# Sixteen weight clamps on POOL, and the partition swaps of one token block as products with an exchanged unit matrix

## The chip, the cores and the metric

The kernel runs on one core of a Trainium2 chip. The metric is device time in microseconds (us) of one launch, the median of several runs. The engines are PE (matrix products, with a queue of its own for weight loads, PEld), DVE, ACT and POOL (elementwise work and reductions), and SP, which here only issues transfers. Each engine works through its own instructions strictly in the order in which the program lists them, and an instruction that waits for another engine holds up everything behind it on its own.

## The reference

```python
def _attn_ref(q, k, v):                      # 8 batches, 8 heads, 576 tokens, head size 64
    q_s = q - np.max(q, axis=-1, keepdims=True)
    q_s = np.exp(q_s)
    q_s = q_s / (np.sum(q_s, axis=-1, keepdims=True) + 1e-09)
    k_s = k - np.max(k, axis=2, keepdims=True)
    k_s = np.exp(k_s)
    k_s = k_s / (np.sum(k_s, axis=2, keepdims=True) + 1e-09)
    kv = np.einsum('bhsd,bhse->bhde', k_s, v)
    return np.einsum('bhsd,bhde->bhse', q_s, kv)

def reference(...):                          # x: 4608 tokens x 512
    x = attn_out.transpose(0, 2, 1, 3).reshape(B * S, H * D)
    x = relu(x @ w_in) ** 2 @ w_out          # 512 -> 2048 -> 512
    return relu(x @ w_in2) ** 2 @ w_out2     # the same with other weights
```

## The kernel before

The 4608 tokens are cut into 9 blocks j of 512. Linear attention gives each block its x in four parts p (two heads each), and x meets the first weight matrix in 16 chunks f per block; such a chunk is one `h_mm`, twelve products of 128x512. From block 6 on, and in the three later matrix stages, the products are combined in a seven-product scheme instead (stages 2 to 4 of the program). All products use numbers split in a high and a low part, so each operand needs an ACT instruction (high part) and a DVE instruction (low part) before PE can use it.

**Weights of the first layer** (`first_weights`, f = 0 to 15) arrive as 64-bit floats and are put together from two 32-bit words: `load_raw` (transfer on SP, line 137), `low_word` (ACT, line 153), `high_word` (a clamp, line 157), `scaled` (ACT, line 162), `join` (DVE, line 167), then `w_hi` (ACT) and `w_lo` (DVE) split them. The raw words of nine weights lie in three rooms (w5, w6, w7); the other seven reuse these places once a join has freed one.

**Attention of block j, part p** (`attend`): for the keys `k_max` (DVE, lines 313 to 315), `k_all` (a maximum over all partitions on POOL, line 319), `k_sub` (DVE, line 323), `k_exp` (ACT, line 326), `kv_mm` (PE, line 334), `kv_whole` (ACT, line 353). For the queries, from block 1 on, a head's 64 numbers lie on two neighbouring groups of 32 partitions, so maxima and sums of each half must be exchanged between the groups: `q_max` (DVE), `q_swap` (four copies of 32x16 on ACT, line 362), `q_max2` and `q_sub` (DVE), `q_exp` (ACT), `q_sum` (DVE), `s_swap` (again four copies on ACT), `q_norm` and `q_turn` (DVE), and `x_mm` (PE, line 405).

**The order** is not the code's order. Every step is entered with a due time, a cost and the places that it uses (a buffer or one of eight PSUM banks, `ps`); `schedule` plays these through once and writes down, engine by engine, in what order the steps would start. `search` first tries 400 random changes of the early due times on ACT and DVE and keeps those by which chunk 8 of block 2 starts earlier in that plan. So a change of one step's engine or cost reorders everything in the first 200 us.

Of the kernel before, what the change touches and what calls it, by code (L numbers as in the profile page):

```python
# [14 lines left out]
ALU = mybir.AluOpType  # L15
# [33 lines left out]
def linear_attention_two_relu2_ffn(ctx: ExitStack, tc: tile.TileContext, q0, k0, eye, qh, kh, vh, wio, out):  # L49
# [104 lines left out]

    def high_word(f, a, h):
        low, high, byte = views(f, a, h)
        nc.vector.tensor_scalar(out=high, in0=high, scalar1=W_MAX, scalar2=-W_MAX, op0=ALU.min, op1=ALU.max)

    def scaled(f, a, h, new):
        wfs[f, a, h] = new()  # L160
# [196 lines left out]
    def swap(name, src):  # L357
# [4 lines left out]
            nc.scalar.activation(out=t[o:o + 32], in_=src[i:i + 32], func=AF.Copy)  # L362
        return t

    def q_max(j, p):
        m = qmt[j, p] = pool.tile([P, 16, 1], F32, name=f"qm{j}_{p}", tag="qm")
        nc.vector.tensor_reduce(out=m, in_=qt[j, p], axis=AX.X, op=ALU.max)

    def q_swap(j, p):
        qmo[j, p] = swap(f"qmo{j}_{p}", qmt[j, p])  # L370

    def q_max2(j, p):
        m = qmt[j, p]
# [10 lines left out]
        s = qmt[j, p] = pool.tile([P, 16, 1], F32, name=f"qs{j}_{p}", tag="qs")  # L384
        nc.vector.tensor_reduce(out=s, in_=qt[j, p], axis=AX.X, op=ALU.add)

    def s_swap(j, p):
        qso[j, p] = swap(f"qso{j}_{p}", qmt[j, p])

    def q_norm(j, p):  # L390
        q, s = qt[j, p], qmt.pop((j, p))
# [370 lines left out]
    def converted(f, a, h, due, raw, wf):  # L762

        (rp, rnew), (wp, wnew) = raw, wf
        l = dma(due - 8000, lambda: load_raw(f, a, h, rnew), 512, [], [rp], held=10000 if (f, a) == (3, 0) else None)
        late = 2500 if f else 0
        c = op("ACT", act(512) + 40, due - 3000, lambda: low_word(f, a, h), [l], [rp], lag=late)
        g = op("DVE", 430, due - 2900, lambda: high_word(f, a, h), [l], [rp], lag=late, port=True)
        x = op("ACT", act(512) + 40, due - 1900, lambda: scaled(f, a, h, wnew), [g], [rp, wp])
        return op("DVE", 690, due - 700, lambda: join(f, a, h), [c, x], [rp, wp], port=True)  # L770

# [121 lines left out]
    def attend(j, p):  # L893
# [31 lines left out]
        if j == 0:  # L925
            l = start_loads[p]
            mq, sq, qT = Place("qm"), Place("qs"), Place(f"q{p % 2}", parent=qspace)
            bq = Place("ps")
            y = op("DVE", 690, d - 13500, lambda: max0(p), [l["q"]], [mq, room])
            y = op("POOL", gps(400), d - 12500, lambda: sub0(p), [y], [mq, room])  # L930
            y = op("ACT", act(512), d - 10500, lambda: qexp0(p), [y], [room])
            y = op("DVE", 690 + 160 + 250 + 690, d - 9500, lambda: q_norm0(p), [y], [sq, room], port=True)
            y = op("PE", 700, d - 8000, lambda: q_turn0(p, bq), [y, start_eye], [bq, room, beginroom])
            turned.append(y)
            qe = op("ACT", act(512, 1), d - 6500, lambda: q_out0(p, qnew), [y], [qT, bq])
            nm = op("DVE", 360, d - 6000, lambda: kv_norm(0, p), [kvmm], [s, ps])
            wh = kv_done[0, p] = op("ACT", 660, d - 5000, lambda: kv_whole(0, p), [nm, start_eye], [s, ps, beginroom])
            xlast = op("PE", 1150, d - 3000, lambda: x_mm0(p, xb), [wh, qe], [xb, qT, beginroom])
        else:
            q = Place(f"q{side}", parent=qroom)  # L940
            lq = dma(d - 30000, lambda: load_q(j, p, qnew), 256, [], [q])
            qm, qo, qs, so = Place("qm"), Place("qmo"), Place("qs"), Place("qso")
            qT = Place("qT")
            y = op("DVE", 690, d - 22000, lambda: q_max(j, p), [lq], [qm, q])
            y = op("ACT", 900, d - 21000, lambda: q_swap(j, p), [y], [qo, qm])
            y = op("DVE", 170, d - 19500, lambda: q_max2(j, p), [y], [qm, qo], port=True)
            y = op("DVE", dve(512), d - 19000, lambda: q_sub(j, p), [y], [q, qm], port=True)
            y = op("ACT", act(512), d - 17500, lambda: q_exp(j, p), [y], [q])
            y = op("DVE", 690, d - 16000, lambda: q_sum(j, p), [y], [qs, q])
            y = op("ACT", 900, d - 14500, lambda: s_swap(j, p), [y], [so, qs])  # L950
            y = op("DVE", 170 + 250 + 690, d - 13000, lambda: q_norm(j, p), [y], [q, qs, so], port=True)
            y = op("DVE", 710, d - 11500, lambda: q_turn(j, p), [y], [qT, q])
            if own:
                nm = op("DVE", 360, d - 8500, lambda: kv_norm(j, p), [kvmm], [s, ps])
                kv_done[j, p] = op("ACT", 660, d - 7500, lambda: kv_whole(j, p), [nm, start_eye, blank[0], x_done.get((j - 1, p))], [s, ps, beginroom])
            xlast = op("PE", 1250, d - 5500, lambda: x_mm(j, p, xb), [y, kv_done[j - 1, p], kv_done.get((j, p))], [xb, qT, beginroom], lag=SLACK)
            x_done[j, p] = xlast
# [13 lines left out]
    def inner(j, kk, d):  # L971
        quad = Place("qc")
        copies = [op("ACT", act(512, 1), d - 5500 - 12000 * (i == 0), lambda i=i: v_copy(j, kk, i), [halves[j, kk + 2 * i][0]], [quad, halves[j, kk + 2 * i][1]]) for i in range(2)]
        combine(f"v{j}_{kk}", v_rooms[j % 2][kk], d, ("DVE",) * 3, lambda: vq[j, kk], quad, copies, *cf_place("cf"))

    blank = [None]

    def blank_unit():
# [2 lines left out]
    for j in range(NB):  # L981
        for p in range(NP):
            plan(when(0, j) - 25000 - (3 - rank(j, p)) * 12500, lambda j=j, p=p: attend(j, p))
        if j == 0:
            plan(when(0, 0) - 25000, blank_unit)


    stored, y_stored, chunks = {}, {}, {}
# [253 lines left out]
```

## Time and profile before

| what | value |
|---|---|
| median of 3 runs | 1509.36 us (1506.9 to 1509.76) |
| the profiled execution | 1511.11 us, of which the trace's span is 1509.3 us |
| PE busy over the span | 1487.6 us, 99% |
| DVE, ACT, POOL busy | 79%, 64%, 17% |
| granted TensorE clock | 0.999 |

PE is nearly always busy, so the time is PE's work plus the gaps in it. Nearly all gaps lie in the first 62 us; there DVE and ACT are as full as PE, and the transfers too. A line such as L157 is the line of the kernel before; in the changed kernel the lines of the second part stand 13 to 23 lines further down.

### The profile page before, as it was taken

Reading aid. Unit: us, or ns where it says so; the run is one execution under the profiler, and the core shown is the slowest. Engines: PE = TensorE matmul, PEld = TensorE weight load, DVE = VectorE, ACT = ScalarE, POOL = GpSimd, SP = SyncE. Lnnn points to the kernel's source line nnn. Section 1 sums busy time; section 2 is a strip of 40 time slices with the busy share of each in tenths; the row PEclk is TensorE's granted clock in tenths of the full one; section 3 lists DMA queues with packets and bytes.
Section 4 is the critical chain, followed back from the end, with each engine's and each line's share of the span. In section 5 each row is a group of like instructions: output and inputs, shape, how many; then the busy total and the mean of one; then the engine's idle time right before and its main releaser. Section 6 shows DMA issues by size and latency. Waiting matters only on the chain.

```text
span 1509.3 us, 30549 instructions
## 1 busy us (share of the span) xinstructions
PE 1487.6 (99%) x12036; PEld 1414.4 (94%) x12036; DVE 1190.4 (79%) x1823; ACT 971.0 (64%) x1617; POOL 253.6 (17%) x193
## 2 busy tenths in 40 slices
PE   6999999999999999999999999999999999999998
PEld 5788888789999999999999999999999999999998
DVE  7998777899867999999986455444456999999996
ACT  8987767787765666666654788787777443444442
POOL 1001000000110111111113153243311111111110
PEclk9999999999999999999999999999999999999999
DMA  9888989986759444444447677677669644444441
GB/s 368 287 292 319 342 319 336 346 295 204 228 189 328 167 146 138 140 139 140 140 139 273 222 233 257 206 259 249 197 202 325 207 146 136 138 137 138 138 137 55
DMA packets 154144, 326.63 MB, mean 216 GB/s; under 512 B 13072, under 2 KB 84880, under 8 KB 151184
## 3 DMA queue, kind: packets, MB, share of 16 engines
q1 hardware_dynamic: 152128, 300.83, 59.5%
q0 software_dynamic: 1872, 23.86, 4.4%
q8 instruction: 94, 1.54, 0.4%
q14 instruction: 50, 0.41, 0.1%
HBM read 189.63 MB, written 135.00 MB: 215 GB/s over the span
## 4 chain that ended last, share of the span: by engine, by line
PE 90%; DMA 3%; ACT 3%; DVE 2%; issue 1%; POOL 1%; SPq 0%; DVEq 0%; ACTq 0%; POOLq 0%
PE y L448 44%; PE m L448 22%; PE h L448 15%; PE n L448 5%; PE xps L405 2%; PE kvps L334 1%; DMA qx<-w 1%; DMA W<-o 1%; POOL touch L188 0%; ACT w L153 0%; ACT wf L162 0%; DMA w<-w 0%; DMA w<-wio 0%; DMA qc<-w 0%; DMA att<-vh 0%
## 5 line engine op out<-in xcount | busy, mean ns | idle before, releaser
L448 PE MATMUL y<-G,W 128*128 128x256 f32 x3024 | 345.3, 277 | 2.0 <-DVE t L488 2.0
L448 PE MATMUL m<-x,W 128*128 128x256 f32 x3024 | 345.7, 277 | 1.5 <-DMA W<-o 1.5
L448 PEld LDWEIGHTS y<-G,W 128*128 128x128 f32 x3024 | 344.8, 188 | 2.2 <-DVE t L488 2.2
L448 PEld LDWEIGHTS m<-x,W 128*128 128x128 f32 x3024 | 345.1, 188 | 1.7 <-DMA W<-o 1.7
L448 PE MATMUL y<-W,G 128*128 128x256 f32 x3024 | 343.9, 276 | 0.0
L448 PEld LDWEIGHTS y<-W,G 128*128 128x128 f32 x3024 | 343.7, 188 | 0.0
L448 PE MATMUL h<-hl,w 128*128 128x512 f32 x1080 | 259.9, 396 | 3.4 <-DVE w L84 3.4
L448 PEld LDWEIGHTS h<-hl,w 128*128 128x128 f32 x1080 | 200.4, 188 | 49.6 <-DVE w L84 5.7
L479 POOL TENSOR_TENSOR ts<-ts,ts 128x512 f32<-128x512 f32 x61 | 93.5, 1533 | 750.2 <-DVE t L518 460.4
L119 ACT ACTIVATE G<-hl 128x1280 fp32r<-128x1280 f32 (+1 forms) x95 | 86.4, 926 | 115.9 <-PE y L448 65.5
L488 DVE TENSOR_TENSOR t<-m,ts 128x512 f32<-128x512 f32 x72 | 49.1, 688 | 97.5 <-PE m L448 77.9
L125 DVE TENSOR_TENSOR G<-hl,G 128x512 fp32r<-128x512 f32 (+1 forms) x95 | 108.7, 1149 | 16.2 <-ACT G L119 15.2
L448 PE MATMUL n<-v,W 128*128 128x256 f32 x1008 | 120.3, 280 | 0.0
L448 PEld LDWEIGHTS n<-v,W 128*128 128x128 f32 x1008 | 117.1, 188 | 2.1 <-issue 1.7
L491 ACT ACTIVATE t<-t 128x512 f32<-128x512 f32 x96 | 59.8, 628 | 56.2 <-DVE t L488 51.8
L494 ACT ACTIVATE t<-t 128x512 f32<-128x512 f32 x144 | 88.5, 627 | 2.3
L125 DVE TENSOR_TENSOR G<-cf,G 128x1280 fp32r<-128x1280 f32 x51 | 79.7, 1562 | 7.9 <-ACT G L119 7.3
L125 DVE TENSOR_TENSOR G<-att,G 128x1280 fp32r<-128x1280 f32 x49 | 75.9, 1549 | 8.4 <-ACT G L119 7.6
L319 POOL PARTITION_ALL_REDUCE m<-m x28 | 27.0, 964 | 310.5 <-DVE m L315 187.0
L435 ACT ACTIVATE r<-h 128x512 f32<-128x512 f32 x96 | 56.8, 593 | 20.6 <-PE h L448 14.8
L521 POOL TENSOR_TENSOR t<-t,t 128x512 f32<-128x512 f32 x34 | 61.0, 1817 | 42.0 <-DVE t L488 42.0
L119 ACT ACTIVATE G<-cf 128x1280 fp32r<-128x1280 f32 x51 | 64.5, 1265 | 5.6 <-DVE cf L106 5.5
(199 smaller groups left out, 1888.5 us busy)
## 6 DMA issues: line engine op xcount, KB each, us to landing
g<-t SPq DMA_DIRECT2D x192, 256.0 KB, 4.0
hl<-g SPq DMA_DIRECT2D x51, 512.0 KB, 3.8
raw<-wio SPq DMA_DIRECT2D x48, 512.0 KB, 5.3
g<-r SPq DMA_DIRECT2D x96, 256.0 KB, 5.2
W<-o POOLq DMA_DIRECT2D x13, 1792.0 KB, 9.5
y<-t SPq DMA_DIRECT2D x72, 256.0 KB, 2.4
w<-wf SPq DMA_DIRECT2D x64, 256.0 KB, 5.4
o<-S SPq DMA_DIRECT2D x9, 1792.0 KB, 8.3
```

The costliest lines, as they stand in the source:

```text
L119: nc.scalar.activation(out=low[key] if x == 0 and key in low else hls[key][:, 0, r], in_=src, func=AF.Copy)
L125: nc.vector.tensor_tensor(out=hl[:, 1, r], in0=src, in1=f32(hi), op=ALU.subtract)
L319: nc.gpsimd.partition_all_reduce(m[:, 1, :P], m[:, 0, :P], P, bass.bass_isa.ReduceOp.max)
L334: nc.tensor.matmul(ps[j * D:(j + 1) * D, 0:D + 1], k[lo:, c, j * D:(j + 1) * D], v[lo:, c, j, :], start=(c == 0), stop=(c == KC - 1),)
L405: nc.tensor.matmul(ps[:, r], begin[b % 2][p], q[:, r], start=True, stop=True)
L435: nc.scalar.activation(out=r0[j, f].rearrange("p a b -> p (a b)"), in_=m.pop(("h", j, f)), func=AF.Relu)
L448: nc.tensor.matmul(ps, a, b, start=start, stop=True, skip_group_check=True)
L479: (nc.gpsimd if eng == "POOL" else nc.vector).tensor_tensor(out=t[k, "s5"], in0=t[k, "s5"], in1=t[k, "s2"], op=ALU.add)
L488: nc.vector.tensor_tensor(out=temp(k, q), in0=m[k, i], in1=t[k, "s5"], op=ALU.add)
L491: nc.scalar.activation(out=t[k, q], in_=t[k, q], func=AF.Relu)
L494: nc.scalar.activation(out=t[k, q], in_=t[k, q], func=AF.Square)
L521: nc.gpsimd.tensor_tensor(out=t[k, q], in0=t[k, q], in1=t[k, o], op=ALU.add)
```

## The change

Two things. The clamp `high_word` of the first layer's sixteen weights runs on POOL instead of DVE (the other 48 clamps stay on DVE). And in block 1 alone, the exchange of neighbouring partition groups for maxima and sums is done by PE: a product with a unit matrix whose groups of 32 columns are exchanged (`turn`), into a PSUM bank that DVE then reads, in place of four ACT copies each. The exchanged unit matrix is built on POOL by four copies when the unit matrix has landed (`turn_unit`).

```diff
--- before.py
+++ after.py
@@ -154,7 +154,7 @@
 
     def high_word(f, a, h):
         low, high, byte = views(f, a, h)
-        nc.vector.tensor_scalar(out=high, in0=high, scalar1=W_MAX, scalar2=-W_MAX, op0=ALU.min, op1=ALU.max)
+        (nc.vector if f else nc.gpsimd).tensor_scalar(out=high, in0=high, scalar1=W_MAX, scalar2=-W_MAX, op0=ALU.min, op1=ALU.max)
 
     def scaled(f, a, h, new):
         wfs[f, a, h] = new()
@@ -362,12 +362,25 @@
             nc.scalar.activation(out=t[o:o + 32], in_=src[i:i + 32], func=AF.Copy)
         return t
 
+    turned_unit = []
+
+    def turn_unit(new):
+        t = new()
+        turned_unit.append(t)
+        for g in range(4):
+            nc.gpsimd.tensor_copy(t[:, 32 * g:32 * g + 32], unit[0][:, 32 * (g ^ 1):32 * (g ^ 1) + 32])
+
+    def turn(name, src, place):
+        t = wide(place, name)[:, :16]
+        nc.tensor.matmul(t, turned_unit[0], src.rearrange("p a b -> p (a b)"), start=True, stop=True)
+        return t.rearrange("p (a b) -> p a b", b=1)
+
     def q_max(j, p):
         m = qmt[j, p] = pool.tile([P, 16, 1], F32, name=f"qm{j}_{p}", tag="qm")
         nc.vector.tensor_reduce(out=m, in_=qt[j, p], axis=AX.X, op=ALU.max)
 
-    def q_swap(j, p):
-        qmo[j, p] = swap(f"qmo{j}_{p}", qmt[j, p])
+    def q_swap(j, p, place):
+        qmo[j, p] = turn(f"qmt{j}_{p}", qmt[j, p], place) if place else swap(f"qmo{j}_{p}", qmt[j, p])
 
     def q_max2(j, p):
         m = qmt[j, p]
@@ -384,8 +397,8 @@
         s = qmt[j, p] = pool.tile([P, 16, 1], F32, name=f"qs{j}_{p}", tag="qs")
         nc.vector.tensor_reduce(out=s, in_=qt[j, p], axis=AX.X, op=ALU.add)
 
-    def s_swap(j, p):
-        qso[j, p] = swap(f"qso{j}_{p}", qmt[j, p])
+    def s_swap(j, p, place):
+        qso[j, p] = turn(f"qst{j}_{p}", qmt[j, p], place) if place else swap(f"qso{j}_{p}", qmt[j, p])
 
     def q_norm(j, p):
         q, s = qt[j, p], qmt.pop((j, p))
@@ -765,7 +778,7 @@
         l = dma(due - 8000, lambda: load_raw(f, a, h, rnew), 512, [], [rp], held=10000 if (f, a) == (3, 0) else None)
         late = 2500 if f else 0
         c = op("ACT", act(512) + 40, due - 3000, lambda: low_word(f, a, h), [l], [rp], lag=late)
-        g = op("DVE", 430, due - 2900, lambda: high_word(f, a, h), [l], [rp], lag=late, port=True)
+        g = op("DVE", 430, due - 2900, lambda: high_word(f, a, h), [l], [rp], lag=late, port=True) if f else op("POOL", 1000, due - 3600, lambda: high_word(f, a, h), [l], [rp], port=False)
         x = op("ACT", act(512) + 40, due - 1900, lambda: scaled(f, a, h, wnew), [g], [rp, wp])
         return op("DVE", 690, due - 700, lambda: join(f, a, h), [c, x], [rp, wp], port=True)
 
@@ -939,15 +952,17 @@
         else:
             q = Place(f"q{side}", parent=qroom)
             lq = dma(d - 30000, lambda: load_q(j, p, qnew), 256, [], [q])
-            qm, qo, qs, so = Place("qm"), Place("qmo"), Place("qs"), Place("qso")
+            qm, qs = Place("qm"), Place("qs")
+            by = j == 1
+            qo, so = (Place("ps"), Place("ps")) if by else (Place("qmo"), Place("qso"))
             qT = Place("qT")
             y = op("DVE", 690, d - 22000, lambda: q_max(j, p), [lq], [qm, q])
-            y = op("ACT", 900, d - 21000, lambda: q_swap(j, p), [y], [qo, qm])
+            y = op("PE", 200, d - 21000, lambda: q_swap(j, p, qo), [y, unit_turned[0]], [qo, qm, unit_place]) if by else op("ACT", 900, d - 21000, lambda: q_swap(j, p, None), [y], [qo, qm])
             y = op("DVE", 170, d - 19500, lambda: q_max2(j, p), [y], [qm, qo], port=True)
             y = op("DVE", dve(512), d - 19000, lambda: q_sub(j, p), [y], [q, qm], port=True)
             y = op("ACT", act(512), d - 17500, lambda: q_exp(j, p), [y], [q])
             y = op("DVE", 690, d - 16000, lambda: q_sum(j, p), [y], [qs, q])
-            y = op("ACT", 900, d - 14500, lambda: s_swap(j, p), [y], [so, qs])
+            y = op("PE", 200, d - 14500, lambda: s_swap(j, p, so), [y], [so, qs, unit_place]) if by else op("ACT", 900, d - 14500, lambda: s_swap(j, p, None), [y], [so, qs])
             y = op("DVE", 170 + 250 + 690, d - 13000, lambda: q_norm(j, p), [y], [q, qs, so], port=True)
             y = op("DVE", 710, d - 11500, lambda: q_turn(j, p), [y], [qT, q])
             if own:
@@ -973,6 +988,13 @@
         copies = [op("ACT", act(512, 1), d - 5500 - 12000 * (i == 0), lambda i=i: v_copy(j, kk, i), [halves[j, kk + 2 * i][0]], [quad, halves[j, kk + 2 * i][1]]) for i in range(2)]
         combine(f"v{j}_{kk}", v_rooms[j % 2][kk], d, ("DVE",) * 3, lambda: vq[j, kk], quad, copies, *cf_place("cf"))
 
+    unit_place = Place("turn", parent=raw_rooms[0])
+    unit_turned = [None]
+
+    def plan_turn():
+        unit_turned[0] = op("POOL", 900, -70000, lambda: turn_unit(lambda: raw_rooms[0].area(3072, P)), [start_eye], [beginroom, unit_place], port=False)
+        turned.append(unit_turned[0])
+
     blank = [None]
 
     def blank_unit():
@@ -983,6 +1005,7 @@
             plan(when(0, j) - 25000 - (3 - rank(j, p)) * 12500, lambda j=j, p=p: attend(j, p))
         if j == 0:
             plan(when(0, 0) - 25000, blank_unit)
+            plan(-80000, plan_turn)
 
 
     stored, y_stored, chunks = {}, {}, {}
```

On POOL, the part between the reset of the unit matrix (`begin`) and the key maxima of block 1 (`m_0` to `m_3`, one for each part p) stood as follows; a row `ISA` that names no tile sets POOL's configuration for the kind of instruction that follows.

```order
L979 MEMSET begin 128x128
L319 ISA
L319 ISA m_0_579<-m_0_579 128x128
L319 ISA m_1_623<-m_1_623 128x128
L319 ISA m_2_782<-m_2_782 128x128
```

In the changed kernel (L157 is the clamp; w_0_222, w_0_251 and w_0_262 are the rooms w5, w6, w7 with the raw words), from the tenth clamp on:

```order
L157 TENSOR_SCALAR w_0_222<-w_0_222 128x512
L319 ISA
L319 ISA m_0_569<-m_0_569 128x128
L157 ISA
L157 TENSOR_SCALAR w_0_222<-w_0_222 128x512
L319 ISA
L319 ISA m_1_589<-m_1_589 128x128
L157 ISA
L157 TENSOR_SCALAR w_0_222<-w_0_222 128x512
L157 TENSOR_SCALAR w_0_251<-w_0_251 128x512 x3
L157 TENSOR_SCALAR w_0_262<-w_0_262 128x512
L319 ISA
```

The first key maximum is now behind the tenth clamp, the second behind the eleventh, the third behind five more, and where one such row served all 28 key maxima, five now stand between the tenth clamp and the third maximum.

On DVE, around the second `k_sub` (`att_2_423` holds the keys of part 1; `qm`, `qs` are maxima and sums, `qmt` the exchanged maxima in PSUM), before:

```order
L315 TENSOR_TENSOR m_1_623<-m_1_623,att_2_432 128x128
L367 TENSOR_REDUCE qm_1_628<-qx_318 128x16
L385 TENSOR_REDUCE qs_0_632<-qx_318 128x16
L157 TENSOR_SCALAR w_0_233<-w_0_233 128x512
L323 TENSOR_TENSOR att_2_432<-att_2_432,m_1_623 128x640
```

and now:

```order
L315 TENSOR_TENSOR m_1_589<-m_1_589,att_2_423 128x128
L323 TENSOR_TENSOR att_2_364<-att_2_364,m_0_569 128x640
L380 TENSOR_REDUCE qm_0_608<-qx_325 128x16
L323 TENSOR_TENSOR att_2_423<-att_2_423,m_1_589 128x640
L387 TENSOR_TENSOR qm_0_608<-qm_0_608,qmt_0_617 128x16
L391 TENSOR_TENSOR qx_325<-qx_325,qm_0_608 128x512
L380 TENSOR_REDUCE qm_1_638<-qx_325 128x16
L398 TENSOR_REDUCE qs_0_644<-qx_325 128x16
```

The sums `qs_0` stood ahead of the second `k_sub` (L323) and now stand behind it. ACT's matching steps have moved the same way: `k_exp` of part 1 now stands directly ahead of `q_exp` of part 0.

On PE, after the first chunks of block 0 (`h_...`), the exchange products L375 of the changed kernel:

```order
L461 MATMUL h_4_593<-hl_0_379,w_0_508 128x512 x9
L461 MATMUL h_4_593<-hl_0_475,w_0_508 128x512 x3
L375 MATMUL qmt_0_617<-qm_0_608,w_0_222 128x16
L461 MATMUL h_5_619<-hl_0_379,w_0_508 128x512 x9
L461 MATMUL h_5_619<-hl_0_475,w_0_508 128x512 x3
L334 MATMUL kvps_0_648<-att_2_364 64x65 x10
L375 MATMUL qst_0_661<-qs_0_644,w_0_222 128x16
L375 MATMUL qmt_1_669<-qm_1_638,w_0_222 128x16
L461 MATMUL h_6_674<-hl_0_379,w_0_562 128x512 x9
```

Eight such products are new; `qst_0` stands behind six chunks and one `kv_mm`, and everything else of PE behind it. Before, `kv_mm` of part 0 was followed by a chunk.

## Rows read from the trace of the kernel before

**Rows 1.** The page's head: busy time and share of each engine.
```profile
span 1509.3 us, 30549 instructions
PE 1487.6 (99%) x12036; PEld 1414.4 (94%) x12036; DVE 1190.4 (79%) x1823; ACT 971.0 (64%) x1617; POOL 253.6 (17%) x193
```
**Rows 2.** Busy time in three stretches: length, PE, PEld, DVE, ACT, POOL, clock, DMA.
```profile
0.00:26.55 26.55, 15.50 (x124) 10.29 (x124) 19.43 (x45) 19.31 (x40) 5.44 (x11) 1.00 0.94 351
26.55:62.00 35.45, 33.14 (x168) 24.81 (x168) 31.84 (x69) 33.20 (x75) 2.44 (x3) 1.00 0.95 356
62.00:110.00 48.00, 47.99 (x288) 38.20 (x289) 46.46 (x103) 42.60 (x107) 3.51 (x4) 1.00 0.77 260
```
**Rows 3.** PE in order of time: start, us, what, and the wait before it.
```profile
26.55 5.78 PE L448 MATMUL h<-hl,w 128*128 128x512 f32 x24 [1.53 <-DVE w L84]
32.64 11.17 PE L448 MATMUL h<-hl,w 128*128 128x512 f32 x48 [0.31 <-DVE w L84]
43.74 0.95 PE L334 MATMUL kvps<-att 128*64 128x65 f32 x20
44.62 3.02 PE L448 MATMUL h<-hl,w 128*128 128x512 f32 x12
48.44 0.43 PE L405 MATMUL xps<-qT,begin 128*128 128x64 f32 x2
```
**Rows 4.** DVE's clamps, grouped, in the first 110 us; and in two stretches.
```profile
L157 DVE TENSOR_SCALAR w<-w 128x512 f32<-128x512 f32 x16 | 6.2, 420 | 0.0
0.00:26.55 26.55, 2.19 (x6) 1.00 0.94 351
26.55:62.00 35.45, 4.13 (x11) 1.00 0.95 356
```
**Rows 5.** One of ACT's swaps (line 362), four copies.
```profile
38.17 0.89 ACT L362 ACTIVATE qmo<-qm 32x16 f32<-32x16 f32 x4 [0.62 <-DVE qm L367]
```
**Rows 6.** POOL in order of time.
```profile
0.73 0.52 POOL L1165 MEMSET begin<- 128x512 f32 x1 [0.29 <-POOLq L1234]
1.19 0.42 POOL L1166 MEMSET begin<- 128x384 f32 x1
5.82 1.05 POOL L263 TENSOR_TENSOR w<-w,mq 128x512 f32<-128x512 f32 x1 [4.21 <-DVE mq L255]
21.91 0.20 POOL L979 MEMSET begin<- 128x128 f32 x1 [5.89 <-PE qps L299]
39.34 0.73 POOL L319 PARTITION_ALL_REDUCE m<-m  x1 [17.22 <-DVE qm L374]
42.69 0.70 POOL L319 PARTITION_ALL_REDUCE m<-m  x1 [2.62 <-DVE m L315]
```
**Rows 7.** POOL's sequencer at lines 263, 319 and 479: duration, first and last start.
```profile
L263 POOLq MODIFY_POOL_CONFIG  x2: 11/14/16, 1.8 to 1.8; - x2
L319 POOLq MODIFY_POOL_CONFIG  x2: 11/11/11, 22.1 to 22.1; - x2
L479 POOLq MODIFY_POOL_CONFIG  x2: 88/88/88, 359.6 to 359.6; - x2
```
**Rows 8.** SP's issue of the tenth raw weight, and issues with KB, us to landing.
```profile
26.26 0.33 SPq L137 DMA_DIRECT2D w<-wio  x1
w<-wio SPq DMA_DIRECT2D x1, 512.0 KB, 7.0
raw<-wio SPq DMA_DIRECT2D x48, 512.0 KB, 5.3
begin<-eye SPq DMA_DIRECT2D x1, 64.0 KB, 1.8
```
**Rows 9.** DVE and ACT in order of time around the first key maximum.
```profile
38.82 0.29 DVE L315 TENSOR_TENSOR m<-m,att 128x128 f32<-128x128 f32 x1
40.10 0.83 DVE L323 TENSOR_TENSOR att<-att,m 128x640 f32<-128x640 f32 x1 [0.83 <-POOL m L319]
40.84 0.68 DVE L378 TENSOR_TENSOR qx<-qx,qm 128x512 f32<-128x512 f32 x1
40.96 0.74 ACT L326 ACTIVATE att<-att 128x640 f32<-128x640 f32 x1 [0.71 <-DVE att L323]
41.60 0.61 ACT L381 ACTIVATE qx<-qx 128x512 f32<-128x512 f32 x1
```
**Rows 10.** Small products and weight loads on PE, grouped.
```profile
L405 PE MATMUL xps<-qT,begin 128*128 128x64 f32 x8 | 1.5, 273 | 0.0
L299 PEld LDWEIGHTS qps<-begin,w x16: 139/142/231, 10.7 to 21.5; 128*128 128x128 f32 x16
```

## The prediction

> **What bounds the kernel now.** I read the page's head first: PE is busy for 1487.6 of 1509.3 us [rows 1]. The three stretches then show where its gaps are: 11.05 us of them before the first chunk at 26.55, 2.31 us from there to 62, and 0.01 us from 62 to 110 [rows 2]. After 62 us nothing but PE's own work counts. Before it, DVE and ACT are nearly full (31.84 and 33.20 of 35.45 us between 26.55 and 62), and so are the transfers (0.95) [rows 2]; POOL, with 2.44 us, is empty there. PE in order of time says what the gaps wait for: weights' low parts from DVE [rows 3]. So the change can save at most the gaps before 62 us, and it can cost whatever it makes PE wait.
>
> **What it removes.** Sixteen clamps of 0.42 us leave DVE: 2.19 us before the first chunk and 4.13 us (with one clamp of a later layer, which stays) up to 62 [rows 4]. Eight swaps of 0.89 us leave ACT [rows 5]. Neither engine ends the span; the relief is worth, at most, the waits that it shortens. Of the 2.31 us of gaps after the first chunk, 0.31 lie before 43.74 [rows 2, 3]; I let the other 2.0 vanish, since both reliefs are larger: −2.0. Before the first chunk I count nothing: the chain there goes through ACT, which does the same low words, scalings and high parts as before.
>
> **What it adds on PE.** Eight products with 16 columns. The nearest row has 64 columns: four `x_mm` pieces, two records each, 1.5 us, so 0.37 each; the floor is two weight loads of 0.14, 0.28 [rows 10]. I take 0.33, and 0.3 for the first, which stands inside the sum below: 0.3 and 7 × 0.33 = +2.3.
>
> **What it adds on POOL.** A one-input instruction over 128x512 is not in the trace on POOL. Writing alone (memset) takes 0.52, two inputs take 1.05 [rows 6]; I take 0.8 for a clamp. Ten clamps at 0.8 are hidden: their words arrive before 34 us, and POOL did nothing between 22.1 and 39.34 [rows 6]. The four copies that build the exchanged matrix wait for the unit matrix (issued about 0.7, 1.8 us to land [rows 8]), so the first subtraction on POOL moves back. With 0.2 per copy (a memset of this width took 0.20 [rows 6]) POOL is free at 3.3 instead of 1.6. If the configuration then takes the 4.0 us priced below, the subtraction starts at 7.4 instead of 5.82; ACT's exponential of it would wait some 0.7. Bounds 0 and 0.7; I take +0.4.
>
> **The switches.** Each row without a tile in POOL's order appears in the trace as MODIFY_POOL_CONFIG: before the first elementwise instruction (1.8 us), before the first key maximum (22.1) and before the first sum of a later stage (359.6) [rows 7]. Their own 11 to 88 ns say nothing of how long POOL then can't work. What bounds it: the first instruction behind it began at 5.82, so the first switch took at most 4.0 us; the second at most 17.2 (22.1 to 39.34) [rows 6, 7]. The lower bound is nothing, since in each case the operand came last and hid the switch. The changed order has five switches between the tenth clamp and the third key maximum, two of them between the first and the second maximum, each with work waiting. I price one by the tighter row, 4.0, stretched by 7.0/5.3, the time in which the same 512 KB load lands in this crowded stretch against its median [rows 8], as code has to be fetched too: 5.3 us. Ends: 0 and 17.2.
>
> The Trainium skill has a rule on just this: "GPSIMD Engine Reference", section "2.1 Instruction dispatch", says that the first call of a freshly loaded kernel on POOL additionally pays about 6 us (measured there as 5.95), with no instruction of its own in a profile. Rows 6 contradict it as a fixed price, since the first switch here fitted into 4.0; by 5.95 the sum below would be +13.3 instead of +11.4.
>
> **The walk.** The tenth raw weight is issued at 26.26 and lands 7.0 later, at 33.3 [rows 8]; its clamp ends at 34.1. The switch behind it ends at 34.1 + 5.3 = 39.4. The operand of the first maximum is ready as before (39.1 [rows 9]), so the first maximum starts at 39.4, as before (39.34). It lasts 0.73 [rows 6]. Then come switch, clamp, switch: 5.3 + 0.8 + 5.3. The second maximum starts at 51.5, where it started at 42.69 before [rows 6]. Behind it, from the first maximum's rows: DVE's `k_sub` begins 0.76 after the maximum's start (39.34 to 40.10), occupies DVE for 0.74, and ACT's `k_exp` begins 0.86 after it [rows 9]. The order now puts the first part's `q_max2`, `q_sub`, `q_sum` on DVE behind this `k_sub`, and `q_exp` on ACT behind this `k_exp`. So: `k_sub` at 52.3, `q_max2` 53.0, `q_sub` 53.2 to 53.9, `q_exp` to 54.5, `q_sum` to 55.3. PE's `qst_0` needs that sum. PE reaches it after six chunks (43.74 before [rows 3]), one `kv_mm` of 0.88 and `qmt_0` of 0.3: at 44.9. It waits 55.3 − 44.9 = +10.4, with everything behind it.
>
> What is late next? DVE and ACT have been held at the same place for about as long, so the three start again together. The next two switches and five clamps end at 51.5 + 0.73 + 5.3 + 5 × 0.8 + 5.3 = 66.8, for the third maximum. DVE gets to its operand 36 instructions behind `k_sub`; at 31.84/69 = 0.46 each [rows 2] that is 52.3 + 16.6 = 68.9: hidden, by 2 us. The clamp that ACT needs first is ready at 59.1, and ACT gets there 18 instructions at 0.44 [rows 2] behind `k_exp`, at 61: hidden too. Without that cover (a switch over 7 us) the third wait comes on top.
>
> **Sum.** 0.3 + 10.4 + 2.3 − 2.0 + 0.4 = +11.4 us. The profiled execution took 1511.11, which gives 1522.5; the median of the runs lies 1.75 lower, so 1509.4 + 11.4 = **1520.8** is what I forecast for the median. A switch of 2.5 us gives a second maximum at 45.9 and +5.6, so 1515; one of 8 us moves the first maximum to 42.1, the second to 59.6, and gives +19.5, so 1529.
>
> **Rivals.**
> *Long switches.* All 16 DMA engines are full while the switches run [rows 2], and the only row under such load allows up to 17.2 us. At 12 us the first maximum starts at 46.1, the second at 71.6, PE goes on at 75.4: a wait of 30.5, +31.5, 1541. For it speaks the load, against it the 4.0 of the first switch.
> *Cheap switches.* The trace never shows POOL waiting for one. At 1 us the second maximum starts at 42.8 and PE waits 1.7: +2.3, 1511.7. No change then, unless PE, now in line behind DVE's maxima and sums at eight places, waits some 1 us at six of them: 1517.
> *Faster.* The switches cost at most 0.4 us each, and the relief reaches PE whole: all 2.31 us of gaps and the 2.19 us of clamps before the first chunk vanish, and the products cost one exposed weight load of 0.14 each, 1.1: −3.4, 1506.0. It decides from the price of a switch alone: above 0.4 us the second maximum is later than PE needs it. DVE at 90% and ACT at 94% speak for some such gain [rows 2]; against it, a PE that had only 2.31 us to gain there.
>
> **Chances.** Switches of 2.5 to 8 us: 0.58 (1514 to 1529). Long ones: 0.15. Cheap ones: 0.17 (1508.5 to 1517), of which a good 0.04 end over 0.2%. Faster: 0.10. What a measurement of this kernel can tell from no change is about 0.2%, 3 us; so faster 0.09, same 0.14, slower 0.77. The range of 1509 to 1535 leaves out most of the faster case and the upper two thirds of the long switches, together about 0.2.
>
> **What would show it.** Right: more MODIFY_POOL_CONFIG rows on POOL between 33 and 70 us, some 5 us of nothing behind each although its operand is there; the second maximum near 51; PE idle for about 10 us before a product of line 375, released by DVE's `qs`; DVE and ACT idle at the same time; after 75 us the same rows as before, shifted. Wrong: the second maximum near 42 and no gap there; or gaps of over 8 us, with a second stall at the third maximum. Were the gap there and the total still small, the start before 26.55 must have become shorter, which I gave nothing.

## The result, and the profile after

| | before | after |
|---|---|---|
| median of 4 runs each, us | 1508.39 (1506.90 to 1509.76) | 1525.62 (1523.36 to 1527.61) |
| ratio, 95% interval | 1 | 1.0102 [1.0071, 1.0133] |
| the profiled execution, us | 1511.11, span 1509.3 | 1527.28, span 1525.3 |

The change costs 1525.62 − 1508.39 = 17.2 us by the medians, and 1508.39 × 0.0102 = 15.4 us by the ratio. The forecast was 1520.8. Slower was right, by the mechanism forecast, and inside the range; the size was too small. Beside each of the later experiments, 4 of the 15 to 19 runs of the kernel before lie at 1515.6 to 1520.9 us, at no lower clock and from no known cause; ratios and medians differ there by up to 0.24%.

Busy time of the changed kernel in the middle stretch of [rows 2] and in three short ones within it (length, PE, PEld, DVE, ACT, POOL, clock, DMA share, GB/s):

```profile
26.55:62.00 35.45, 21.30 (x96) 16.11 (x94) 14.59 (x29) 16.57 (x32) 4.39 (x5) 0.81 0.60 231
35.00:43.00 8.00, 5.15 (x23) 3.94 (x21) 3.62 (x9) 3.04 (x6) 0.00 (x0) 1.00 1.04 391
43.00:51.00 8.00, 5.50 (x14) 4.23 (x14) 1.42 (x2) 2.26 (x4) 0.73 (x2) 0.63 0.49 191
51.00:57.50 6.50, 1.55 (x21) 1.03 (x20) 0.00 (x0) 0.00 (x0) 0.65 (x2) 0.76 0.00 0
```

Between 26.55 and 62 us PE is busy for 21.30 us, where it was 33.14 [rows 2]. DVE and ACT have fallen with it, from 31.84 and 33.20 to 14.59 and 16.57, and the transfers from 0.95 to 0.60. POOL gained only 1.95 us of busy time. So all engines stood still together, for something that counts as nobody's work: between 51 and 57.5 us DVE and ACT have not one instruction, and not a byte moves. POOL in order of time, from the tenth clamp on (compare [rows 6]):

```profile
33.76 1.12 POOL L157 TENSOR_SCALAR w<-w 128x512 f32<-128x512 f32 x1 [5.91 <-ACT w L222]
43.18 0.72 POOL L319 PARTITION_ALL_REDUCE m<-m  x1 [8.30 <-DMA w<-wio]
50.99 0.64 POOL L157 TENSOR_SCALAR w<-w 128x512 f32<-128x512 f32 x1 [7.09 <-issue]
57.49 0.72 POOL L319 PARTITION_ALL_REDUCE m<-m  x1 [5.86 <-issue]
65.08 3.55 POOL L157 TENSOR_SCALAR w<-w 128x512 f32<-128x512 f32 x5 [6.87 <-issue]
78.65 0.99 POOL L319 PARTITION_ALL_REDUCE m<-m  x1 [10.03 <-DVE m L315]
```

"<-issue" means that POOL waited for nothing that the profile shows. Each such gap has a row of POOL's sequencer at its start. At lines 157 and 319 (first and last start at the right):

```profile
L157 POOLq MODIFY_POOL_CONFIG  x4: 98/98/98, 43.9 to 58.2; - x4
L319 POOLq MODIFY_POOL_CONFIG  x6: 1/33/36, 34.8 to 68.8; - x6
```

Four switches stand between the tenth clamp and the five later ones: 8.30, 7.09, 5.86 and 6.87 us. The 8.30 is put down to a transfer, but the operand of the first maximum was ready at 38.06, and that of the second at 39.05, when DVE's last steps on them ended. The second maximum starts at 57.49, where it started at 42.69. DVE's second `k_sub` follows it:

```profile
58.24 0.83 DVE L323 TENSOR_TENSOR att<-att,m 128x640 f32<-128x640 f32 x1 [12.89 <-POOL m L319]
```

PE waits twice for what follows from these maxima (compare [rows 3]; some rows in between are left out):

```profile
25.34 14.81 PE L461 MATMUL h<-hl,w 128*128 128x512 f32 x60
45.50 0.58 PE L375 MATMUL qmt<-qm,w 128*128 128x16 f32 x2 [5.35 <-DVE qm L380]
45.92 5.47 PE L461 MATMUL h<-hl,w 128*128 128x512 f32 x12
61.31 0.61 PE L375 MATMUL qst<-qs,w 128*128 128x16 f32 x2 [8.76 <-DVE kvs L347]
62.19 4.60 PE L461 MATMUL h<-hl,w 128*128 128x512 f32 x12
112.47 0.95 PE L334 MATMUL kvps<-att 128*64 128x65 f32 x20 [1.32 <-ACT att L326]
```

The chunks behind the two waits take 5.47 and 4.60 us where a chunk took 3.02 [rows 3]. The granted clock is still 1.00 from 35 to 43 us and 0.63 from 43 to 51, so much of the first chunk ran at the lower of the two levels, 1.2 instead of 2.4 GHz.

How much of this reaches the end? The first product of the next matrix stage (`n`) is a milestone. The group of these products before and after, with the first and last start at the right:

```profile
L448 PE MATMUL n<-v,W x1008: 276/276/682, 341.9 to 472.1; 128*128 128x256 f32 x168
```
```profile
L461 PE MATMUL n<-v,W x1008: 276/276/682, 362.2 to 493.7; 128*128 128x256 f32 x168
```

It starts 20.3 us later, but the span is only 16.0 longer. The other 4.3 come back late. From the first `n` product on, PE waits 3.9 us in before and 1.1 in after, and its busy time is 1.5 us shorter (1159.1 against 1157.6). So it isn't quite true that nearly all gaps of before lie in the first 62 us: 13.4 us of PE's idle time lie there, 3.9 lie in three late waits, and 4.4 behind its last product. Its two long late waits, by line:

```profile
PE y L448 <- DVE t L488: 2.0, 1, 2.0
PE m L448 <- DMA W<-o: 1.5, 1, 1.5
```

### The profile page after: what moved, and what is told of

It is laid out like the page before. It is cut to its first block, busy times and chain, and to the rows that moved or that the text cites. A ratio compares the mean times of both kernels' runs of the same rounds, so it can differ in the third digit from the quotient of the medians.

```text
span 1525.3 us, 30566 instructions
## 1 busy us (share of the span) xinstructions
PE 1494.4 (98%) x12052; PEld 1420.1 (93%) x12052; DVE 1189.0 (78%) x1807; ACT 964.1 (63%) x1585; POOL 262.0 (17%) x213
## 4 chain that ended last, share of the span: by engine, by line
PE 86%; DMA 5%; DVE 4%; issue 2%; ACT 2%; SPq 0%; POOL 0%; DVEq 0%; ACTq 0%; POOLq 0%
PE y L461 45%; PE m L461 23%; PE h L461 12%; PE n L461 5%; DMA w<-wio 1%; PE xps L418 1%; DMA w<-wf 1%; DMA qc<-w 1%; PE kvps L334 1%; DMA att<-vh 1%; DMA w<-vh 0%; DVE W L125 0%; DMA w<-w 0%; DVE wf L167 0%; DMA w<-q 0%
## 5 line engine op out<-in xcount | busy, mean ns | idle before, releaser
L461 PE MATMUL h<-hl,w 128*128 128x512 f32 x1080 | 266.2, 402 | 0.4 <-DVE w L84 0.4
L461 PEld LDWEIGHTS h<-hl,w 128*128 128x128 f32 x1080 | 204.4, 192 | 46.3 <-issue 0.8
L492 POOL TENSOR_TENSOR ts<-ts,ts 128x512 f32<-128x512 f32 x61 | 90.1, 1477 | 771.9 <-DVE t L531 463.2
```

Of the source, the lines that this page charges most:

```text
L461: nc.tensor.matmul(ps, a, b, start=start, stop=True, skip_group_check=True)
L492: (nc.gpsimd if eng == "POOL" else nc.vector).tensor_tensor(out=t[k, "s5"], in0=t[k, "s5"], in1=t[k, "s2"], op=ALU.add)
```

## The experiments

The theory at the start: the loss is the delay of the second key maximum by the switches of POOL. The rivals: the clamps themselves or their relief of DVE (any order with them is slow), the products on PE with their queues behind DVE, and the clock that falls in PE's waits (a cost of its own that could be had back). The median of before, run beside each, was 1508.4 to 1509.0.

**1. The same order without the late clamps on POOL.** PE's order is that of after, to the instruction; only the seven clamps that need the switches are issued on DVE.

```diff
-        (nc.vector if f else nc.gpsimd).tensor_scalar(out=high, ...
+        (nc.vector if f or a + NPAIR * h > 8 else nc.gpsimd).tensor_scalar(out=high, ...
```

> The changed kernel in its own planned order, with the seven clamps that stand behind the first key maximum given to DVE, so that POOL needs one switch in place of five; every other engine keeps its order, and the exchange products stay. Theory (the switches between clamps and key maxima hold PE, and the pause lowers its clock): second key maximum at 41 to 44 us, no wait of PE over 1.5 us between 26 and 110, granted clock 1.00, 1507 to 1511 us. Rival (the new order or the products in PE's queue are what costs): waits of PE at lines 375 stay, 1520 us or more. Rival (clamps on POOL are slow beside DVE): half of the loss stays with nine clamps on POOL, 1515 to 1518 us.

Measured: 1508.84 us, ratio 0.9998 [0.9982, 1.0015]. POOL and PE in order of time:

```profile
38.94 0.73 POOL L319 PARTITION_ALL_REDUCE m<-m  x1 [12.35 <-DMA w<-wf]
40.44 1.13 POOL L319 PARTITION_ALL_REDUCE m<-m  x1 [0.77 <-issue]
```
```profile
41.75 0.37 PE L375 MATMUL qmt<-qm,w 128*128 128x16 f32 x2 [1.25 <-DVE qm L380]
41.96 3.01 PE L461 MATMUL h<-hl,w 128*128 128x512 f32 x12
95.29 0.95 PE L334 MATMUL kvps<-att 128*64 128x65 f32 x20 [1.30 <-ACT att L326]
```

By the median, the whole loss is gone with the late switches. The second maximum stands 57.49 − 40.44 = 17.05 us earlier than in after, and the first `n` product 362.2 − 345.0 = 17.2: one for one. Nine clamps on POOL, all products on PE and the new order stay and cost nothing that the median shows; at the first `n` product 345.0 − 341.9 = 3.1 us of the 20.3 are still there, 1.30 of them at the last row shown.

**2. The switches alone, in the kernel before.** All clamps on DVE, all swaps on ACT; a one-column clamp on POOL behind each of the first two key maxima of block 1 makes POOL switch to and fro. Its result is used by nothing.

```diff
         nc.gpsimd.partition_all_reduce(m[:, 1, :P], m[:, 0, :P], P, bass.bass_isa.ReduceOp.max)
+        if b == 1 and p < 2:
+            one = pool.tile([P, 1], F32, name=f"one{p}", tag="margin")
+            nc.gpsimd.tensor_scalar(out=one, in0=m[:, 1, :1], scalar1=W_MAX, scalar2=-W_MAX, op0=ALU.min, op1=ALU.max)
```

> The kernel before with nothing of the change but two one-column clamps on POOL, behind the first and the second key maximum of block 1: four more switches, no work worth naming. Theory: each switch takes 5.6 to 8.4 us as in the changed kernel; the second maximum moves from 42.7 to some 54, the third from 56.8 to some 69, PE waits 6 to 12 us in all and its clock falls: 1516 to 1525 us. Rival (switches cost little, the order does): 1507 to 1511 us, maxima at the old times.

Measured: 1521.74 us, ratio 1.0109 [1.0069, 1.0148]. POOL in order of time:

```profile
39.52 0.73 POOL L319 PARTITION_ALL_REDUCE m<-m  x1 [17.23 <-DVE qm L377]
48.18 0.18 POOL L322 TENSOR_SCALAR one<-m 128x1 f32<-128x1 f32 x1 [7.94 <-issue]
54.09 0.72 POOL L319 PARTITION_ALL_REDUCE m<-m  x1 [5.74 <-issue]
```

Two instructions of 0.18 us, with four switches around them, cost as much as the whole change by the ratio (1.0109 against 1.0102), and three quarters of it by the medians, 1521.74 − 1508.41 = 13.3 us apart. The second maximum is 11.4 us later than in [rows 6], and PE waits 7.75 and 4.44 us at the `kv_mm` and `x_mm` behind it. The price lies in the switches and not in the clamps.

**3 and 4. PE kept busy in its waits.** Is the clock a cost of its own? Products on data already there, into the bank that the exchange then overwrites, fill the two waits: 20 ahead of `qmt_0`, and 34 ahead of `qst_0` in the first kernel, 44 in the second. They add work and leave none out.

```diff
-        t = wide(place, name)[:, :16]
+        whole = wide(place, name)
+        for _ in range({"qmt1_0": 20, "qst1_0": 34}.get(name, 0)):
+            nc.tensor.matmul(whole, w0[2][:, 0, :P], w0[2][:, 0], start=True, stop=True)
+        t = whole[:, :16]
```

> The changed kernel with idle products put on PE where it waits: 20 of 512 columns ahead of the first exchange product, 34 ahead of the second (some 4.6 and 7.8 us of work for waits of 5.4 and 8.8); results unchanged. Theory (the wait costs a second time through the clock, which the trace grants at 0.81 between 26.55 and 62): granted clock 1.00 there, the chunk behind each wait back to 3.0 us from 5.5 and 4.6, and 4 to 5 us less than the changed kernel, 1520 to 1522 us. Rival (these chunks are slow since their operands come late): the same 1524 to 1527 us as the changed kernel, chunks still 4.6 to 5.5 us long; over 1527 if the fill delays PE.

> As the run with filled waits, but with 44 idle products ahead of the second exchange product instead of 34, since 2.8 us of that wait were left and the chunk behind it still took 4.5 us. Theory (a pause of a few us costs again through the clock): the chunk behind the second wait at 3.0 us, PE 1.5 us further on at 100 us than with the shorter fill, clock 1.00 to 62 us. The first fill should still be worth nothing, since the time at which PE goes on is set by POOL: so at most 2 us under the changed kernel up to 110 us. Rival (the chunk is slow because its operands come late): still 4.5 us.

Measured: 1528.65 us, ratio 1.0141 [1.0124, 1.0158], and 1527.61, ratio 1.0138 [1.0124, 1.0152]. PE of the second, in order of time:

```profile
45.24 2.97 PE L464 MATMUL h<-hl,w 128*128 128x512 f32 x12
49.02 10.27 PE L376 MATMUL qst<-w 128*128 128x512 f32 x44
60.76 0.39 PE L378 MATMUL qst<-qs,w 128*128 128x16 f32 x2 [1.46 <-DVE kvs L347]
61.22 2.99 PE L464 MATMUL h<-hl,w 128*128 128x512 f32 x12
67.55 0.40 PE L378 MATMUL qst<-qs,w 128*128 128x16 f32 x2 [1.28 <-DVE qs L401]
68.69 7.33 PE L464 MATMUL h<-hl,w 128*128 128x512 f32 x24 [0.75 <-DVE w L84]
101.04 0.95 PE L334 MATMUL kvps<-att 128*64 128x65 f32 x20
```

Both chunks are back at 2.97 and 2.99 us, with a granted clock of 1.00 up to 62 us. Yet nothing is won: PE arrives too early at the next products that need POOL, DVE and ACT, waits there (1.28, 0.75), and two chunks then take 7.33, at a granted clock of 0.79 from 68 to 76 us, where after took 5.71 at 1.00. The `kv_mm` that stands at 101.04 here stood at 100.05 in after. With the shorter fill it stands at 98.58, 1.5 us earlier than in after, but there the second maximum came 1.65 earlier too (55.84), and the second chunk still took 4.51. So in neither kernel was the chunks' loss to the clock had back: PE is held at other engines' results behind the second maximum. My expectation of a gain was wrong.

The first `n` product starts at 360.7 and 362.3, where after had 362.2. That both kernels nevertheless end above the 1525.62 of after thus arises later; in their profiles PE waits 1.9 and 2.5 us for a transfer there, which after does not. Why, no run tests; and the profiled execution of the second is 3.8 us above its median.

**5. One late clamp on DVE.** The eleventh alone, which stood between the first two maxima; the order is that of after, and one switch to the five clamps and one back remain behind the second maximum.

```diff
+        (nc.vector if f or a + NPAIR * h == 10 else nc.gpsimd).tensor_scalar(out=high, ...
```

> The changed kernel in its own order, with one clamp alone, the eleventh, given to DVE: the second key maximum follows the first without the two switches, the first switch and the two around the last five clamps stay. Theory (the two switches between the maxima are the long wait): second maximum within 2 us of the first, the wait of 8.8 us at the second exchange product gone, the one of 5.4 us at the first (the switch ahead of the first maximum) still there; 1513 to 1517 us. Rival (PE's queue order makes the wait at the sums): it stays at 5 us or more, 1520 us or more. Third maximum some 18 us after the second; if PE then waits for it, a new wait of 1 to 3 us at 65 to 70.

Measured: 1513.23 us, ratio 1.0042 [1.0027, 1.0057]. POOL in order of time:

```profile
32.95 0.68 POOL L157 TENSOR_SCALAR w<-w 128x512 f32<-128x512 f32 x1 [6.40 <-DMA w<-wio]
40.24 1.43 POOL L319 PARTITION_ALL_REDUCE m<-m  x2 [6.61 <-DMA w<-wf]
49.60 4.68 POOL L157 TENSOR_SCALAR w<-w 128x512 f32<-128x512 f32 x5 [7.93 <-DMA g<-r]
```

This single instruction carries 1525.62 − 1513.23 = 12.4 of the 17.2 us: without it two switches between the maxima vanish, and with them the wait of 8.76 at `qst_0` (0.53 are left at `qst_1`). The first switch, behind the tenth clamp, remains: PE waits 2.68 us at `qmt_0`, where it waits 1.25 in run 1, and the chunk behind takes 4.28. But of the 4.8 us by which the first `n` product is late here (346.7), run 1 has 3.1 without any late switch, so some 1.7 are left for the three switches that remain.

**6. The parts alone, and fewer clamps in a new order.** The products with all clamps on DVE; the clamps with all swaps on ACT; and both parts with the first nine clamps only on POOL, where the planner knows of it. In all three the order is made anew. The clamps alone are the diff of the change without its second part.

The products alone:

```diff
-        (nc.vector if f else nc.gpsimd).tensor_scalar(out=high, ...
+        nc.vector.tensor_scalar(out=high, ...
```

Nine clamps, in the code as in run 1, and in the plan:

```diff
-        ... if f else op("POOL", 1000, due - 3600, lambda: high_word(f, a, h), ...
+        ... if f or a + NPAIR * h > 8 else op("POOL", 1000, due - 3600, lambda: high_word(f, a, h), ...
```

> The changed kernel with all clamps back on DVE: the exchange products alone, in the order that the planner then writes. Theory: eight products of 0.13 to 0.3 us and swaps gone from ACT, no switches: 1506 to 1511 us. Rival (PE waits in its queue behind DVE's maxima and sums): waits at lines 375 of 1 us each or more, 1512 to 1518 us.

> The exchange products alone a second time, with more rounds, since 0.9973 with an interval of 0.9947 to 0.9999 does not yet say that it beats the kernel before. If the gain is real: 1506 to 1508 us, ratio 0.997 to 0.999. If it was chance: ratio 0.999 to 1.001.

> The other part alone: all sixteen clamps on POOL, the swaps of block 1 on ACT as before, planned anew. Its order has a switch to clamps behind each of the first three key maxima, seven switches in all ahead of the fourth. Theory: second maximum 13 to 16 us behind the first, third another 15 to 18 us, fourth 13 to 16 us; 1522 to 1532 us. Rival (without exchange products PE's queue stays free): under 1515 us.

> Both parts of the change, but only the first nine clamps on POOL, planned anew; one switch stands ahead of all key maxima. Theory (POOL's clamps cost nothing where they need no switch, and spare DVE 3.8 us before the first chunk): first chunk 0.5 to 1.5 us before 26.5, 1504 to 1508 us, as good as the exchange products alone or 1 us better. Rival (the relief is worth nothing, ACT sets the start): 1507 to 1510 us. 1512 or more would speak for POOL's clamps slowing DVE.

| | median us | ratio, 95% interval |
|---|---|---|
| products alone | 1507.30 | 0.9973 [0.9947, 0.9999] |
| products alone, again | 1507.20 | 0.9974 [0.9957, 0.9992] |
| clamps alone | 1532.87 | 1.0134 [1.0093, 1.0176] |
| nine clamps and products | 1507.40 | 0.9981 [0.9959, 1.0003] |

The clamps alone lose as much as both parts, or more. In their order of POOL, four key maxima have switches between them (two rows of clamps, ahead of the last two maxima, are left out):

```profile
38.98 0.96 POOL L319 PARTITION_ALL_REDUCE m<-m  x1 [11.40 <-DMA w<-wf]
48.18 1.26 POOL L157 TENSOR_SCALAR w<-w 128x512 f32<-128x512 f32 x2 [8.23 <-issue]
56.11 0.72 POOL L319 PARTITION_ALL_REDUCE m<-m  x1 [6.67 <-issue]
74.57 0.72 POOL L319 PARTITION_ALL_REDUCE m<-m  x1 [6.90 <-ACT r L435]
89.34 0.72 POOL L319 PARTITION_ALL_REDUCE m<-m  x1 [5.90 <-issue]
```

The products alone are faster than before by some 0.26% by the ratio, and the only version whose interval leaves out 1 on that side; by the medians they gain only 1.1 and 1.8 us, 0.07% and 0.12% (before: 1508.41 and 1508.96). Its first `n` product starts at 342.3, 0.4 us behind that of before: the early stages gain nothing. In its profile PE has none of before's two late waits of 2.0 and 1.5 us. Whether and why the early order decides on these late waits I didn't test; and the profiled execution of before is 2.7 us above its median, so that a part of them may belong to that execution. With nine clamps and the products the first chunk starts at 28.47 and not, as I expected, ahead of 26.5: DVE's relief didn't bring the start forward there.

**7. The switch by itself.** A kernel of its own, with none of this kernel's work: elementwise instructions and partition maxima on POOL alone, in equal rows and in turns, then the same turns while 1 MB loads fill the DMA engines. A second kernel ends with an elementwise instruction instead of a maximum, and has a third set of turns beside stores.

```diff
+    def elementwise():
+        nc.gpsimd.tensor_scalar(out=m[:, 0], in0=m[:, 1], scalar1=2.0, scalar2=-2.0, op0=ALU.min, op1=ALU.max)
+
+    def maximum():
+        nc.gpsimd.partition_all_reduce(m[:, 1], m[:, 0], P, bass.bass_isa.ReduceOp.max)
+
+    def alternate():
+        for _ in range(6):
+            elementwise()
+            maximum()
```

> None of the reference's work: POOL alone does six clamps of 128x128, then six maxima over partitions, then the two in turn six times with nothing else running, then the same six times while 40 loads of 1 MB keep the DMA engines full; the output is zeros. Theory (a switch makes POOL fetch code, 5.6 to 7.1 us in the changed kernel): 6 to 8 us from the end of one to the start of the other in turn, under 0.5 us between equal ones. If transfers slow the fetch, the turns under load are longer by 1 us or more; if not, all alike within 0.3 us. Rival (the gaps in the changed kernel are waits for operands that the trace does not show): under 1 us in turn, too.

> POOL alone again, none of the reference's work, output zeros. Against the run with switches alone, two things differ: the program's last POOL instruction is a clamp, not a maximum, and a third set of six turns runs while stores, not loads, keep the DMA engines full. Theory (a switch to what POOL holds already fetches nothing, and the program before ends with an elementwise sum, so that its first switch, at most 4.0 us, was an empty one): the first clamp starts within 3 us of the program's start, not at 7.6. Rival (the first switch costs as much as any, 6 to 7 us): again at 7 to 8 us. Under stores: 6 to 7 us as in quiet turns if only reads from memory compete with the fetch, 10 to 12 us if any transfer does.

POOL of the first kernel in order of time: start, a row of equal ones, quiet turns with a copy behind them, turns under loads.

```profile
7.64 2.16 POOL L24 TENSOR_SCALAR m<-m 128x128 f32<-128x128 f32 x6 [7.22 <-issue]
15.66 4.70 POOL L27 PARTITION_ALL_REDUCE m<-m  x6 [5.86 <-issue]
...
96.61 0.28 POOL L24 TENSOR_SCALAR m<-m 128x128 f32<-128x128 f32 x1 [6.76 <-issue]
102.88 0.72 POOL L27 PARTITION_ALL_REDUCE m<-m  x1 [5.99 <-issue]
103.67 0.29 POOL L42 COPY big<-m 128x128 f32<-128x128 f32 x1
...
146.93 0.72 POOL L27 PARTITION_ALL_REDUCE m<-m  x1 [11.30 <-issue]
159.36 0.28 POOL L24 TENSOR_SCALAR m<-m 128x128 f32<-128x128 f32 x1 [11.71 <-issue]
```

And of the second kernel: its start, and two turns beside stores.

```profile
1.20 2.18 POOL L23 TENSOR_SCALAR m<-m 128x128 f32<-128x128 f32 x6 [0.77 <-DVE m L20]
9.00 4.71 POOL L26 PARTITION_ALL_REDUCE m<-m  x6 [5.62 <-issue]
...
242.60 0.28 POOL L23 TENSOR_SCALAR m<-m 128x128 f32<-128x128 f32 x1 [6.96 <-issue]
249.01 0.72 POOL L26 PARTITION_ALL_REDUCE m<-m  x1 [6.13 <-issue]
```

In quiet, a switch to the maximum takes 5.6 to 6.0 us and one back to the clamp 6.8 to 7.1 in the first kernel (up to 7.6 in the second). Six equal instructions in a row have no gap, and neither has a COPY behind a maximum: it starts 0.07 us after the maximum's end, without a row of the sequencer. So not all elementwise work needs the switch. Loads (411 GB/s from 104 to 205 us in the first kernel) stretch the switches that lie wholly under them to 9.1 to 11.7, over both kernels; beside stores (381 GB/s) a switch takes 5.9 to 7.6. And the very first switch went with how the program ends: 7.22 us where the last instruction was a maximum, and nothing to be seen where it was elementwise (0.77, a wait for DVE). The simplest reading is that POOL keeps what it held from one execution to the next; it rests on one execution of each of two programs. The changed kernel fits: it ends with elementwise sums, and its first row of the sequencer stands at 3.42, its first subtraction at 5.93, so its first switch took at most 2.5 us.

## Why the prediction was right, and where its size came from

**The mechanism was right.** More MODIFY_POOL_CONFIG rows between 33 and 70 us: one (shown twice) for each of five switches, at 34.8, 43.9, 51.8, 58.2 and 68.8. PE idle for about 10 us before a product of line 375: 8.76 at `qst_0`, after 5.35 at `qmt_0`. The profile names `kvs` of line 347 as what ended the 8.76; the sum `qs_0`, one instruction ahead of it on DVE, ended at 61.26, and the product starts at 61.31. DVE and ACT idle at the same time: 12.89 us ahead of the second `k_sub` on DVE, 12.00 ahead of the second `k_exp` on ACT. One sign failed: after 75 us the rows are not those of before, shifted, since the order is new there too. Runs 1, 2 and 5 show that the switches ahead of the second maximum carry the loss, from both sides: taken away, added alone, and by halves.

**The step that was mis-sized is the price of the switch: 5.3 us forecast, 8.30, 7.09 and 5.86 measured.** It rested on the first switch of [rows 6, 7], read as "at most 4.0", and on a stretch for the load. Run 7 shows the fault. A first switch to elementwise work was empty where the program ended with such work, and the kernel before does end so, with sums on POOL. The row bounded nothing. The second switch, at a DMA share of 0.49, took 7.09, and the third, with nothing moving, 5.86, which are the quiet times of run 7. The first, with the transfers still full (1.04, 391 GB/s), took 8.30. That loads can stretch a switch is shown by run 7; that they made this one 8.30 is not, since in runs 3, 4 and 5, with the same order on POOL up to there and a DMA share of 1.03 to 1.04 from 34 to 40 us, it took 6.45, 8.23 and 6.61. The second maximum came 57.49 − 51.5 = 6.0 us later than forecast: the tenth clamp ended 0.8 later, at 34.9, then +3.0, +1.8 and +0.6 for the three switches, and −0.2 for the clamp between them (0.64, forecast 0.8).

The Trainium skill, "GPSIMD Engine Reference", section "2.1 Instruction dispatch", gives 5.95 us for the first call of freshly loaded code. The prediction set it aside by that row; the quiet turns to the maximum (5.83 to 5.99 in the first kernel of run 7) agree with it to 0.12 us. It gives no second price for the way back to elementwise work, which was the dearer one in these turns (6.76 to 7.10).

**What else was missing.** The sum held no term for the clock. Of the two slow chunks the first lay inside a wait and cost nothing; the second cost 4.60 − 3.02 = 1.6 (from `qst_0` to the first `n` product it is 300.9 us in after and 299.2 in run 1, where this chunk took 3.01). And PE waits 1.32 us at a `kv_mm` at 112, which comes of the new order, since run 1 has it too (1.30). Up to the first `n` product this closes: 11.4 + 6.0 + 1.6 + 1.3 = 20.3 us, as measured. That it closes to the tenth is luck in part: the 11.4 holds 0.4 for the start, which didn't come, and the sum leaves out the 0.36 us that PE waits at 69.33. Then 4.3 come back in the late stages, which I hadn't counted either, since I read "after 62 us nothing but PE's own work counts" from rows that end at 110; by the medians 17.2 are left.

**The other terms.** The products: 0.29 to 0.40 us long each in the kernel with products alone, but the next product starts 0.13 to 0.25 us after each of them starts, 1.5 us for all eight where 0.3 + 2.3 was forecast. The gaps of 2.31 us behind the first chunk are gone there, near the forecast −2.0, but its first chunk starts 1.3 us later (27.85); at the first `n` product +0.4 are left. In after, where some products ran at the lower clock, the eight take some 2.4. The start: +0.4 forecast for the copies of the exchanged matrix, but the first chunk begins 1.2 us earlier, at 25.34, and the first subtraction on POOL at 5.93, 0.11 later than before; the copies end at 3.2, and the switch behind them takes at most 2.5, not 4.0. The gain went into the wait that follows, whose end POOL sets. The cover of the third maximum held: it waits for DVE (10.03 <-DVE), as forecast. The cover of ACT was said to hold by 2 us and fell short: ACT waits 1.33 us for the first of the five clamps, at 65.75. PE shows 0.36 us of it.

**The rivals.** "Long switches" of 12 us exist under full loads (11.71 in run 7), but not here: the longest took 8.30, and only the first met full transfers. "Cheap switches" and "faster" fell with the price. Their idea that relief reaches PE is borne out at most in the small, by the products alone (0.07% to 0.27%).

## What to carry to other kernels

Count how often an engine changes its kind of work, and price each change by a place where the operand was already there; a switch hidden behind a late operand, or one at a program's start, says nothing of the price. On POOL, put clamps and sums (all that brings a row of the sequencer with it) ahead of the first partition maximum or behind the last one that others wait for: one clamp of 0.64 us in between cost 12.4 us here. And a planner that counts 1 us for such an instruction, with no cost for the change, doesn't see this, as here.

## What was not expected of the hardware

- A switch of POOL's kind of work blocks it for 5.6 to 6.0 us one way (to the maximum over partitions) and 6.8 to 7.6 the other way, with a row of only 1 to 98 ns in the trace, and no traffic on the DMA engines that the profile counts (0 GB/s between 20 and 99 us in the second kernel of run 7). Loads at 411 GB/s stretch it to up to 11.7; stores hardly. A COPY needed no switch behind a maximum (0.07 us).
- POOL seems to hold its configuration across executions: the first switch of a program looked empty if the program ends in the same kind (0.77 against 7.22 us, one execution each).
- A one-input clamp of 128x512 takes 0.64 us on POOL at the least, against 0.42 on DVE [rows 4]; the sixteen of after have a median of 0.66, and two took 1.19 and 1.12.
- Behind waits of 5.35 and 8.76 us, chunks of 3.02 us took 5.47 and 4.60, at a granted clock of 0.81 from 26.55 to 62 us and 0.70 from 62 to 68.
